# ScalarE's rounding of each activation bank put ahead of VectorE's sums of it, with conversions in other slots and some turned rows put off

## The chip, the core and the metric

The kernel runs on one core of one Trainium2 chip. The metric is device microseconds of one execution; the profiler's span, from the first to the last instruction, is a little shorter. Five engines work side by side, each with its own queue in program order: PE (TensorE, matmuls), DVE (VectorE), ACT (ScalarE), POOL (GpSimd) and SP (SyncE, which here only issues DMAs).

## The reference

Three layers follow one another, on 4 batches of 448 tokens of width 768, all in 32-bit floats:

```python
attn = sigmoid(q @ k.T / 8 - log(448)); x = attn @ v              # 12 heads of 64
u  = x + (x.T @ U @ V).T                                          # rank 32
x2 = u + max(u @ w_ch1, 0) @ w_ch2                                # 768 -> 3072 -> 768
th = x2 @ w_theta
y  = w_tok_r @ (x2 * cos(th)) + w_tok_i @ (x2 * sin(th))
out = (x2 + y) + max((x2 + y) @ moe2_w_ch, 0)
```

The weights arrive as 64-bit floats and are turned into 32-bit ones on the chip. Each product of 32-bit operands is made of three passes over rounded high parts and the remainders (low parts): high by high, high by low, low by high. So every operand of TensorE needs a high part, made by ScalarE (`hi_act`, L111, or the `relu` in L862), and a low part, a subtraction on GpSimd (`lo_pool`, L114) or VectorE (`lo_dve`, L120).

## The kernel before

The change lies in the middle layer, `max(u @ w_ch1, 0) @ w_ch2`. The hidden width of 3072 is cut into NB = 12 blocks `i` of 256 channels (two halves `n` of 128), and the batches into two pairs `pr` (batches `2*pr + t`, t = 0 or 1). A phase (i, pr) does two things at once, in seven slots k = 0 to 6. It fills four banks `g` of PSUM with `u @ w_ch1` (24 `fill` calls of three matmuls each, lines L841 to L843, in the order (t, n) = 10, 11, 00, 01), and it does the second product for the phase before it, in `seven`: one product of nine matmuls (L895 to L897) per slot, in Strassen's form with seven products in place of eight. Between them the operands are the activations `a11`, `a12`, `a22` (tiles `h_..a`), their sums `s1` to `s4` (tiles `h_..s`, from the temporary tiles `A` and `B`), and the weights `b11`, `b21`, `b22` and their sums `t1` to `t4`.

TensorE's order is written out: `first_half` calls `after(k)` (the product of slot k), then three to five fills, then `do(i, pr, k)`, the weight conversions that the table `units` gives to the slot. In slot 6 `do` comes ahead of the fills. When a bank `g` is full, `post_10`, `post_11`, `post_00` or `post_01` evacuates it. ScalarE and VectorE never read one bank at the same time: the program puts the two in their order of emission and a semaphore between them.

The products are accumulated in two PSUM tiles `acc_a` and `acc_d` of three banks, which VectorE adds to the result `X` in SBUF (L903, 1344 columns). At k = 0 the new product is also the start of a second sum: ScalarE copies it to the other tile (L918), and the product of k = 1 accumulates there. That product also reads `a12`, which is the bank filled last in the phase before.

A weight conversion (`Conv`) has the steps `size` (ScalarE), three `words` steps on VectorE (L153, L157, L163), and a finish of its own: for `w_ch1` high and low parts; for half of `w_ch2` four sums on VectorE (L258 to L261) and the parts; for `th` two VectorE instructions (L196, L199); for `wc` four subtractions on VectorE (L324 to L327). `place` and `place_extra` give each step its slot (-1 is the last slot of the phase before, 7 and up belong to the next phase). `extra` are conversions that a later layer needs, one per phase: six `th`, six `wc`, seven `tok`. Each takes one of three buffers `ca`.

In the last block (i = 11) the finished parts of `X` are turned for the next layer: `turn` transposes 128x448 elements on VectorE into a staging tile `stg` (L966), which is again one of the three buffers `ca`, and issues a DMA from GpSimd to DRAM (L967). `load_xn` (L1193) reads them back from SP's queue. After the last phase `seven_last` does the last seven products with no fills between them; then come the turned rows of batch 3 (six more, in other buffers) and `project`, the product with `w_theta`, column block c after column block c. Its operand for c = 2, the tile `xl_2`, is made by VectorE (L120) behind all of those turned rows.

Of the kernel before, what the change touches and what calls it, by code (L numbers as in the profile page):

```python
# [15 lines left out]
ALU = mybir.AluOpType  # L16
# [8 lines left out]
def tile_kernel(  # L25
# [16 lines left out]
    B, H, S, D = q.shape  # L42
    DM = H * D
    R = moe_U.shape[1]
    DF = moe_w_ch1.shape[1]
    P = 128
# [181 lines left out]
    def conv_w2(i, n):  # L228
        def dma(s):
            loader().dma_start(  # L230
                out=s.rearrange("p (j c) t -> p j (c t)", j=FB),
                in_=w2_w[i * FB * P:(i + 1) * FB * P, 2 * n * HN:2 * (n + 1) * HN].rearrange("(j p) x -> p j x", p=P),
            )
        name = f"w2_{i}_{n}"
        raw = jobs2.setdefault(i, [])

        def operand(x, home, a):
            w2_t[i, x] = o = ring_op(home, f"w2_{i}_{x}")
            hi_act(o[:, 0], a)
            return o[:, 1], a, o[:, 0]  # L240

        def fin(a, t):
            names = [f"b{j + 1}{n + 1}" for j in range(FB)]
            homes = names if i else [f"t{2 * n + j + 1}" for j in range(FB)]
            los = [operand(x, home, a[:, j * HN:(j + 1) * HN]) for j, (x, home) in enumerate(zip(names, homes))]
            yield
            for lo in los:
                lo_late(*lo)
        if i and n:
            t2 = []  # L250

            def quads():
                return [f(q.A)[:, j * HN:(j + 1) * HN] for q in raw for j in range(FB)]

            def sums():
                b11, b21, b12, b22 = quads()
                t2.append(late["c"].tile([P, HN], F32, tag="t2", name=f"t2_{i}"))
                nc.vector.tensor_sub(b11, b12, b11)  # L258
                nc.vector.tensor_sub(t2[0], b11, b22)
                nc.vector.tensor_sub(b12, b22, b12)  # L260
                nc.vector.tensor_add(b21, b21, t2[0])  # L261

            def ops(*names):
                def go():
                    t1, t4, t3, b22 = quads()
                    got = dict(t1=t1, t2=t2[0], t3=t3, t4=t4, b22=b22)
                    for lo in [operand(x, x, got[x]) for x in names]:
                        lo_pool(*lo)
                return go
            job = Conv(name, P, DM, dma, None, more=[sums, ops("t2", "t1"), ops("t3", "b22", "t4")])  # L270
        else:
            job = Conv(name, P, DM, dma, fin)
        raw.append(job)
        return job
# [382 lines left out]
    def place(i, pr, name, job, *when):  # L657
        queue(name, job)
        size, words, *rest = when
        for k in (size, words, words, words, *rest):  # L660
            ph = 2 * i + pr + k // NT7
            units.setdefault((ph // 2, ph % 2, k % NT7), []).append(name)
        assert len(job.steps) == 4 + len(rest)

    def place_extra(i, pr, k0, k1, k2):
        name, job = extra.pop(0)
        more = (k2,) if len(job.steps) == 5 else (k2, k2 + 1) if len(job.steps) == 6 else (k2, k2 + 1, k2 + 3, k2 + 4)
        place(i, pr, name, job, k0, k1, *more)

    for i in range(NB):  # L670
        if i:
            place(i, 0, ("w2", i, 0), conv_w2(i, 0), -1, 0, 2)
            place(i, 0, ("w2", i, 1), conv_w2(i, 1), 0, 1, 4, 5, 6)
            if extra:
                place_extra(i, 0, 2, 3, 6)
        if i == L:
            break
        place(i, 1, ("w1", i + 1, 0), conv_w1(i + 1, 0), 0, 1, 2)
        place(i, 1, ("w1", i + 1, 1), conv_w1(i + 1, 1), 1, 2, 6)
        if i and extra:  # L680
            place_extra(i, 1, 3, 4, 6)
# [175 lines left out]
    def max0(out, src, in1, op):  # L857
        nc.vector.scalar_tensor_tensor(out=out, in0=src, scalar=0.0, in1=in1, op0=ALU.max, op1=op)  # L858
# [32 lines left out]
    def product(o, i, pr, a, b, start):  # L891
# [5 lines left out]
            nc.tensor.matmul(o[:, e], wl, h[:, 0], start=False, stop=True, skip_group_check=True)  # L897
        h_free((i, pr, a))

    def add(i, pr, t, n, o, final):  # L900
        b = 2 * pr + t
        x = X[:, n * K3:(n + 1) * K3, b * S:(b + 1) * S]
        nc.vector.tensor_add(x, o, x)  # L903
        if final and i == L and b < B - 1:
            for d in range(n * K3, (n + 1) * K3):
                turn(b, d)

    seeded = []

# [59 lines left out]
    def turn(b, d):  # L969
        turn_x(b, d, cv.tile([P, DM], F32, tag="ca", name=f"stg_{b}_{d}", bufs=3))  # L970
# [17 lines left out]
        nc.scalar.activation(temp("A", i, pr), g, AF.Relu)  # L988

    def post_11(i, pr, g):  # L990
        max0(temp("B", i, pr), g, part["A"], ALU.add)
        relu((i, pr, "a22"), g)
        split_s(i, pr, "s1", "B", lo_pool)

    def post_00(i, pr, g):
        max0(part["A"], g, part["A"], ALU.subtract)
        max0(part["B"], g, part["B"], ALU.subtract)
        relu((i, pr, "a11"), g)
        split_s(i, pr, "s2", "B", lo_pool)

    def post_01(i, pr, g):
        max0(part["B"], g, part["B"], ALU.add)
        relu((i, pr, "a12"), g)

    ORDER = ((1, 0, post_10), (1, 1, post_11), (0, 0, post_00), (0, 1, post_01))

    def first_half(i, pr, after):

        def fills():
            for t, n, post in ORDER:  # L1010
                g = bank_g(f"{i}_{pr}_{t}{n}")
                for c in range(NK):
                    fill(i, pr, t, n, *divmod(c, K3), g)
                    if c == NK - 1:
                        post(i, pr, g)
                    yield
        todo = fills()
        for k, n in enumerate((5, 3, 3, 3, 3, 3, 4)):
            after(k)
            if k == 6:  # L1020
                do(i, pr, k)
            for _ in range(n):
                next(todo)
            if k < 6:
                do(i, pr, k)

    def phase(i, pr, prev):
        last = (i, pr) == (L, 1)

        def after(k):  # L1030
            if prev[0] == 0:
                if k < 6:
                    Y(*prev, *divmod(k, K3), lambda e2: None)
                return
            seven(*prev, k)
            if k == 0:
                split_s(*prev, "s3", "A", lo_dve)
            if k == 1:
                split_s(*prev, "s4", "B", lo_pool)
            if last and k == 6:  # L1040
                load_th(1)
                split_x(0)
        first_half(i, pr, after)
        if last:
            load_th(2)
# [95 lines left out]
    def tail(k):  # L1141
        if k == 0:
            split_s(*prev, "s4", "B", lo_pool)
        elif k == 1:
            split_s(*prev, "s3", "A", lo_dve)
            load_th(3, "b11", "t1")
            split_x(1)
        elif k == 3:
            load_th(4, "t2", "b22")
        elif k == 5:  # L1150
            load_th(5, "t3", "b21")
    seven_last(*prev, tail)
    c_st.close()
    s_st.close()
# [493 lines left out]
```

## Time and profile before

| | us |
|---|---|
| median of 3 runs | 1169.35 (1168.2 to 1170.58) |
| the profiled execution, its own time | 1169.59 |
| its span | 1167.8 |
| TensorE (matmul) busy | 1104.8, 95% of the span |
| VectorE busy | 888.3, 76% |
| ScalarE busy | 465.7, 40% |
| GpSimd busy | 413.4, 35% |

A busy share is an average over layers with different limits. The middle layer's phases run from about 240 us to 891 us of the span: those that carry `th` up to 406, those that carry `wc` up to 599, those that carry `tok` up to 794, and the rest behind them. TensorE's idle time, 63 us in all, lies mostly in the first two of these. The mean granted clock of TensorE over the span is 0.981.

### The profile page before, as it was taken

The page shows a single profiled execution, that of the slowest core. Times are in us where ns is not written, and L with a number is a line of the kernel's source. Part 1 is how long each engine was busy: PE and PEld are TensorE (multiplying, and loading weights), DVE is VectorE, ACT ScalarE, POOL GpSimd, SP SyncE. Part 2 cuts the span into 40 slices and gives each one's busy share as a digit, 9 for nine tenths or more (in the row PEclk, how much of TensorE's full clock was granted, in tenths as well). Part 3 has the DMA queues.
Part 4 walks back from the last instruction along what each step waited for, and adds up shares of the span by engine and source line. Part 5 has one row for each costly group of instructions (what it writes and reads, how often), then busy time and mean ns, then how long its engine had stood idle before and what let it go on. Part 6 is the DMA issues. An engine that isn't in the chain of part 4 may idle for free.

```text
span 1167.8 us, 16419 instructions
## 1 busy us (share of the span) xinstructions
PE 1104.8 (95%) x6165; PEld 962.8 (82%) x6165; DVE 888.3 (76%) x1127; ACT 465.7 (40%) x724; POOL 413.4 (35%) x409
## 2 busy tenths in 40 slices
PE   8999988999898999888899999999998999999997
PEld 5455567988787888787788999999987999999997
DVE  5788775588787898888888888887777663644884
ACT  6787752223333323333333333334311632542330
POOL 6421125132333243344444343434332332230373
PEclk9999998999999999999999999999999999999999
DMA  9998422123232324334243323232038432080433
GB/s 167 153 181 144 100 70 86 55 83 126 68 130 82 108 95 135 122 108 138 81 139 99 110 86 98 77 112 70 28 127 255 122 48 34 10 275 28 95 62 75
DMA packets 219919, 122.06 MB, mean 105 GB/s; under 512 B 166064, under 2 KB 205424, under 8 KB 219712
## 3 DMA queue, kind: packets, MB, share of 16 engines
q1 hardware_dynamic: 207728, 99.68, 33.5%
q0 software_dynamic: 8256, 20.87, 6.4%
q8 instruction: 48, 0.79, 0.3%
q10 hardware_dynamic: 3856, 0.48, 0.3%
q14 instruction: 31, 0.25, 0.1%
HBM read 91.23 MB, written 28.38 MB: 102 GB/s over the span
## 4 chain that ended last, share of the span: by engine, by line
PE 50%; DVE 36%; issue 6%; ACT 5%; SPq 2%; DMA 1%; POOL 1%; DVEq 0%; POOLq 0%; ACTq 0%
DVE X L903 12%; PE av L563 3%; DVE ws_w L157 3%; PE sc L529 3%; PE y L1296 3%; PE y L1294 3%; PE y L1295 3%; PE g L841 3%; DVE ws_w L153 3%; PE g L842 3%; PE g L843 3%; DVE ca_w L163 3%; PE th L1184 2%; PE th L1182 2%; PE th L1181 2%
## 5 line engine op out<-in xcount | busy, mean ns | idle before, releaser
L841 PE MATMUL g<-a,w 128*128 128x448 f32 x576 | 212.2, 368 | 3.6 <-DVE h L858 3.6
L842 PE MATMUL g<-a,w 128*128 128x448 f32 x576 | 211.5, 367 | 0.0
L843 PE MATMUL g<-a,w 128*128 128x448 f32 x576 | 211.0, 366 | 0.0
L114 POOL TENSOR_TENSOR h_s<-B,h_s 128x448 fp32r<-128x448 f32 x66 | 80.9, 1226 | 363.2 <-ACT h_s L111 363.2
L862 ACT ACTIVATE h_a<-g 128x448 fp32r<-128x448 f32 x66 | 35.8, 543 | 333.0 <-DVE B L858 295.0
L841 PEld LDWEIGHTS g<-a,w 128*128 128x128 f32 x576 | 111.0, 193 | 12.9 <-DVE h L858 3.9
L903 DVE TENSOR_TENSOR X<-acc_d,X 128x1344 f32<-128x1344 f32 x67 | 103.9, 1550 | 19.9 <-PE acc_d L897 19.8
L842 PEld LDWEIGHTS g<-a,w 128*128 128x128 f32 x576 | 110.5, 192 | 7.7
L843 PEld LDWEIGHTS g<-a,w 128*128 128x128 f32 x576 | 110.0, 191 | 7.6
L903 DVE TENSOR_TENSOR X<-acc_a,X 128x1344 f32<-128x1344 f32 x67 | 103.8, 1550 | 2.6 <-PE acc_a L897 2.0
L511 ACT ACTIVATE A<-sc,bias_s 128x896 f32<-128x896 f32 x72 | 70.0, 1015 | 14.6 <-PE sc L529 14.6
L858 DVE SCALAR_TENSOR_TENSOR h_a<-g,h_a 128x448 fp32r<-128x448 f32 x66 | 41.2, 624 | 43.9 <-ACT h_a L862 43.9
L114 POOL TENSOR_TENSOR zl<-t,zh 128x768 fp32r<-128x768 f32 x21 | 40.6, 1953 | 87.9 <-ACT zh L111 62.6
L1296 PE MATMUL y<-tok,zl 128*128 128x448 f32 x168 | 61.1, 363 | 0.0
L1294 PE MATMUL y<-tok,zh 128*128 128x448 f32 x168 | 60.8, 362 | 0.0
L1295 PE MATMUL y<-tok,zh 128*128 128x448 f32 x168 | 60.7, 362 | 0.0
L563 PE MATMUL av<-A,v 128*64 128x448 f32 x288 | 59.4, 548 | 0.7 <-ACT A L511 0.7
L163 DVE SCALAR_TENSOR_TENSOR ca_w<-ca_w,ws_w 128x768 uint32<-128x768 uint32 x48 | 56.8, 1183 | 3.8 <-DVE ws_w L157 0.5
L114 POOL TENSOR_TENSOR w<-ca_w,w 128x768 fp32r<-128x768 f32 x22 | 41.1, 1870 | 52.1 <-ACT w L111 52.1
L157 DVE SCALAR_TENSOR_TENSOR ws_w<-ca_w,ws_w 128x768 uint32<-128x768 uint32 x48 | 53.0, 1105 | 4.1
L1302 DVE TENSOR_TENSOR X<-y,X 128x448 f32<-128x448 f32 (+2 forms) x36 | 15.6, 464 | 52.3 <-PE y L1296 52.1
L1463 POOL DMA_DIRECT2D out_dram<-o x45 | 27.5, 618 | 63.4 <-DVE o L1474 60.4
(308 smaller groups left out, 2847.7 us busy)
## 6 DMA issues: line engine op xcount, KB each, us to landing
ws_w<-in_moe_w_ch_dram SPq DMA_DIRECT2D x42, 768.0 KB, 4.4
x_d<-stg POOLq DMA_DIRECT2D x24, 224.0 KB, 3.9
q<-in_q_dram SPq DMA_DIRECT2D x90, 56.0 KB, 4.3
xn<-x_d SPq DMA_DIRECT2D x52, 96.0 KB, 2.9
k<-in_k_dram SPq DMA_DIRECT2D x86, 56.0 KB, 4.4
v<-in_v_dram POOLq DMA_DIRECT2D x12, 384.0 KB, 5.0
ws_w<-in_moe_w_ch_dram POOLq DMA_DIRECT2D x6, 768.0 KB, 6.1
ws_th<-in_moe_w_theta_dram SPq DMA_DIRECT2D x6, 768.0 KB, 4.2
```

What stands on the lines that cost most here:

```text
L114: nc.gpsimd.tensor_sub(o, a, b)
L157: nc.vector.scalar_tensor_tensor(out=lw, in0=A, scalar=0x80000000, in1=lw, op0=ALU.bitwise_and, op1=ALU.bitwise_or)
L163: nc.vector.scalar_tensor_tensor(out=A if self.dest is None else self.dest(), in0=A, scalar=3, in1=lw, op0=ALU.logical_shift_left, op1=ALU ...
L511: nc.scalar.activation(a, ps, AF.Sigmoid, bias=bias_s, scale=SCALE)
L563: nc.tensor.matmul(ps[h * D:(h + 1) * D, :S], v_t[p // 2][:, 2 * (p % 2) + h, c, :], A_t[p, c][:, h, :], start=c == 0, stop=False,)
L841: nc.tensor.matmul(o, wh, xh, start=(kh, kk) == (0, 0), stop=False, skip_group_check=True)
L842: nc.tensor.matmul(o, wh, xl, start=False, stop=False, skip_group_check=True)
L843: nc.tensor.matmul(o, wl, xh, start=False, stop=(kh, kk) == (1, K3 - 1), skip_group_check=True)
L903: nc.vector.tensor_add(x, o, x)
L1294: nc.tensor.matmul(o, zh[:, sl], tok_h[:, i, :], start=first and n == 0, stop=False)
L1295: nc.tensor.matmul(o, zh[:, sl], tok_l[:, i, :], start=False, stop=False)
L1296: nc.tensor.matmul(o, zl[:, sl], tok_h[:, i, :], start=False, stop=last and n == len(slots) - 1)
```

## The change

It has five parts.

1. In `post_11`, `post_00` and `post_01` ScalarE's `relu` of the bank is emitted ahead of VectorE's sums of the same bank (`max0`); the sums are passed to `relu` as what it does in between. In `post_00` the sum `B` also comes ahead of `A`.
2. The low part of `s3` is made by GpSimd (`lo_pool`), where VectorE made it; not so in `tail`, which belongs to `seven_last`.
3. The conversions' steps take other slots: the second half of `w_ch2` goes from size 0, words 1 to size 1, words 2; the extra conversion of pair 0 from size 2, words 3, finish 6 to size 5, words 6, finish 7 (slot 0 of the next phase); the finish of the first `w_ch1` half from slot 2 to slot 3.
4. The order of the last three parts of `w_ch2` is t4, t3, b22.
5. A turned row is no longer made right behind its last sum: it goes on a list, `pending`. Two of the list are made at the end of each slot 0 to 5, and all that are left when `seven_last` has done its last sum.

```diff
-            job = Conv(name, P, DM, dma, None, more=[sums, ops("t2", "t1"), ops("t3", "b22", "t4")])
+            job = Conv(name, P, DM, dma, None, more=[sums, ops("t2", "t1"), ops("t4", "t3", "b22")])
...
-            place(i, 0, ("w2", i, 1), conv_w2(i, 1), 0, 1, 4, 5, 6)
+            place(i, 0, ("w2", i, 1), conv_w2(i, 1), 1, 2, 4, 5, 6)
             if extra:
-                place_extra(i, 0, 2, 3, 6)
+                place_extra(i, 0, 5, 6, 7)
...
-        place(i, 1, ("w1", i + 1, 0), conv_w1(i + 1, 0), 0, 1, 2)
+        place(i, 1, ("w1", i + 1, 0), conv_w1(i + 1, 0), 0, 1, 3)
...
+    pending = []
+
+    def turns(n):
+        for key in pending[:n]:
+            turn(*key)
+        del pending[:n]
...
         if final and i == L and b < B - 1:
-            for d in range(n * K3, (n + 1) * K3):
-                turn(b, d)
+            pending.extend((b, d) for d in range(n * K3, (n + 1) * K3))
...
     def post_11(i, pr, g):
-        max0(temp("B", i, pr), g, part["A"], ALU.add)
-        relu((i, pr, "a22"), g)
+        relu((i, pr, "a22"), g, lambda: max0(temp("B", i, pr), g, part["A"], ALU.add))
         split_s(i, pr, "s1", "B", lo_pool)
 
     def post_00(i, pr, g):
-        max0(part["A"], g, part["A"], ALU.subtract)
-        max0(part["B"], g, part["B"], ALU.subtract)
-        relu((i, pr, "a11"), g)
+        def sums():
+            for x in "BA":
+                max0(part[x], g, part[x], ALU.subtract)
+        relu((i, pr, "a11"), g, sums)
         split_s(i, pr, "s2", "B", lo_pool)
 
     def post_01(i, pr, g):
-        max0(part["B"], g, part["B"], ALU.add)
-        relu((i, pr, "a12"), g)
+        relu((i, pr, "a12"), g, lambda: max0(part["B"], g, part["B"], ALU.add))
...
             if k < 6:
                 do(i, pr, k)
+                turns(2)
...
             if k == 0:
-                split_s(*prev, "s3", "A", lo_dve)
+                split_s(*prev, "s3", "A", lo_pool)
...
+        elif k == 6:
+            turns(len(pending))
     seven_last(*prev, tail)
```

VectorE's queue at the end of phase (6, 0), from the evacuation of the bank `g_0_00` to that of `g_0_01`; before, with the semaphores that each row waits for:

```order
L858 SCALAR_TENSOR_TENSOR A_0_4821<-g_0_00_4886,A_0_4821 128x448 [waits PE_49]
L858 SCALAR_TENSOR_TENSOR B_0_4878<-g_0_00_4886,B_0_4878 128x448 [waits Pool_49]
L858 SCALAR_TENSOR_TENSOR h_0_a_4939<-g_0_00_4886,h_0_a_4939 128x448 [waits Activation_49]
L903 TENSOR_TENSOR X<-acc_d,X 128x3x448 [waits PE_49]
L324 TENSOR_TENSOR sp_wc_0_t<-ca_wc_0_4863 128x192 [waits DMAHW1_49]
L325 TENSOR_TENSOR sp_wc_0_t<-ca_wc_0_4863,sp_wc_0_t 128x192 [waits DVE_49]
L326 TENSOR_TENSOR sp_wc_0_t<-ca_wc_0_4863 128x192
L327 TENSOR_TENSOR sp_wc_0_t<-ca_wc_0_4863,sp_wc_0_t 128x192 [waits DVE_49]
L858 SCALAR_TENSOR_TENSOR B_0_4878<-g_0_01_4945,B_0_4878 128x448 [waits PE_49,Pool_49]
L858 SCALAR_TENSOR_TENSOR h_0_a_4998<-g_0_01_4945,h_0_a_4998 128x448 [waits Activation_49]
```

The same place of the changed kernel:

```order
L858 SCALAR_TENSOR_TENSOR B_0_4878<-g_0_00_4884,B_0_4878 128x448 [waits Activation_49,Pool_49]
L858 SCALAR_TENSOR_TENSOR A_0_4819<-g_0_00_4884,A_0_4819 128x448
L858 SCALAR_TENSOR_TENSOR h_0_a_4930<-g_0_00_4884,h_0_a_4930 128x448
L910 TENSOR_TENSOR X<-acc_d,X 128x3x448 [waits PE_49]
L153 TENSOR_SCALAR ws_wc_0_4800<-ws_wc_0_4800 128x768 [waits DMAHW6_49,DMAHW5_49]
L157 SCALAR_TENSOR_TENSOR ws_wc_0_4800<-ca_wc_0_4951,ws_wc_0_4800 128x768 [waits DVE_49,Activation_49]
L163 SCALAR_TENSOR_TENSOR ca_wc_0_4951<-ca_wc_0_4951,ws_wc_0_4800 128x768 [waits DMAHW4_49,DVE_49]
L858 SCALAR_TENSOR_TENSOR B_0_4878<-g_0_01_4938,B_0_4878 128x448 [waits Activation_49,Pool_49]
L858 SCALAR_TENSOR_TENSOR h_0_a_4989<-g_0_01_4938,h_0_a_4989 128x448
L324 TENSOR_TENSOR sp_wc_0_t<-ca_wc_0_4951 128x192 [waits DMAHW1_49,DVE_49]
```

The first sum of a bank now waits for ScalarE and the low part behind it for nothing. Between the last sum of the second product and the bank `g_0_01` the three words steps of `wc` stand where its four subtractions stood; these follow the bank.

ScalarE's queue at the same place (`w_6_..` are parts of `w_ch2`), before:

```order
L862 ACTIVATE h_0_a_4939<-g_0_00_4886 128x448 [waits DVE_49,PE_49]
L111 ACTIVATE h_0_s_4942<-B_0_4878 128x448 [waits PE_49,Pool_49]
L111 ACTIVATE w_6_t_4952<-t_6_4919 128x384
L111 ACTIVATE w_6_t_4954<-ca_w_6_0_4748 128x384
L111 ACTIVATE w_6_t_4968<-ca_w_6_1_4803 128x384
L111 ACTIVATE w_6_b_4970<-ca_w_6_1_4803 128x384
L111 ACTIVATE w_6_t_4972<-ca_w_6_0_4748 128x384 [waits PE_49]
L111 ACTIVATE sp_wc_0_b<-ca_wc_0_4863 128x768 [waits DMAHW0_49,Pool_49]
L862 ACTIVATE h_0_a_4998<-g_0_01_4945 128x448 [waits DVE_49]
```

And in the changed kernel:

```order
L862 ACTIVATE h_0_a_4930<-g_0_00_4884 128x448 [waits PE_49]
L111 ACTIVATE h_0_s_4935<-B_0_4878 128x448 [waits DVE_49]
L111 ACTIVATE w_6_t_4945<-t_6_4912 128x384
L111 ACTIVATE w_6_t_4947<-ca_w_6_0_4748 128x384
L149 ACTIVATE ca_wc_0_4951<-ws_wc_0_4800 128x768 [waits DMAHW6_49,DMAHW5_49,DMAHW4_49]
L111 ACTIVATE w_6_t_4963<-ca_w_6_0_4748 128x384 [waits PE_49]
L111 ACTIVATE w_6_t_4965<-ca_w_6_1_4828 128x384
L111 ACTIVATE w_6_b_4967<-ca_w_6_1_4828 128x384
L862 ACTIVATE h_0_a_4989<-g_0_01_4938 128x448 [waits PE_49]
```

The rounding of the bank waits for TensorE alone; ScalarE's wait for VectorE stands at the rounding of the sum `B` behind it. Behind the last row comes the copy L918 in both.

VectorE's queue at the end of `seven_last`, from the third last sum; before:

```order
L903 TENSOR_TENSOR X<-acc_d,X 128x3x448 [waits PE_49]
L903 TENSOR_TENSOR X<-acc_a,X 128x3x448 [waits PE_49]
L966 STREAM_TRANSPOSE stg_0_7488<-X 128x448 [waits DMASW2_49,DVE_49]
L966 STREAM_TRANSPOSE stg_1_7491<-X 128x448 [waits DMASW3_49]
L966 STREAM_TRANSPOSE stg_2_7494<-X 128x448 [waits DMASW4_49]
L903 TENSOR_TENSOR X<-acc_d,X 128x3x448 [waits PE_49]
L1169 MEMSET half_pi 128x1
L966 STREAM_TRANSPOSE stg_7540<-X 128x448 [waits DMASW5_49,DVE_49]
```

And in the changed kernel, from the last sum:

```order
L910 TENSOR_TENSOR X<-acc_d,X 128x3x448 [waits PE_49]
L972 STREAM_TRANSPOSE stg_4_7478<-X 128x448 [waits DMASW2_49]
L972 STREAM_TRANSPOSE stg_5_7481<-X 128x448 [waits DMASW3_49]
L972 STREAM_TRANSPOSE stg_0_7484<-X 128x448 [waits DMASW4_49]
L972 STREAM_TRANSPOSE stg_1_7487<-X 128x448 [waits DMASW5_49,DVE_49]
L972 STREAM_TRANSPOSE stg_2_7490<-X 128x448 [waits DMASW6_49,DVE_49]
L972 STREAM_TRANSPOSE stg_3_7493<-X 128x448 [waits DMASW7_49,DVE_49]
L972 STREAM_TRANSPOSE stg_4_7496<-X 128x448 [waits DMASW0_49,DVE_49]
L972 STREAM_TRANSPOSE stg_5_7499<-X 128x448 [waits DMASW1_49,DVE_49]
L972 STREAM_TRANSPOSE stg_0_7502<-X 128x448 [waits DMASW2_49,DVE_49]
L972 STREAM_TRANSPOSE stg_1_7505<-X 128x448 [waits DMASW3_49,DVE_49]
L972 STREAM_TRANSPOSE stg_2_7508<-X 128x448 [waits DMASW4_49,DVE_49]
```

Eleven turned rows now stand behind the last sum, in three staging buffers, so that from the fourth on each waits for the DMA of the row three before it. Six turned rows of batch 3 and then `xl_2` follow in both kernels; the first of the six waits for the DMA of one of the last rows (DMASW5 before, DMASW6 after, the tenth of the eleven).

## Rows read from the trace of the kernel before

**Rows 1.** The page's part 1, busy time and share of the span.

```profile
PE 1104.8 (95%) x6165; PEld 962.8 (82%) x6165; DVE 888.3 (76%) x1127; ACT 465.7 (40%) x724; POOL 413.4 (35%) x409
```

**Rows 2.** Waits of TensorE: total us, times, longest us.

```profile
PE acc_d L895 <- ACT acc_d L918: 14.6, 5, 2.9
PE acc_a L895 <- ACT acc_a L918: 9.9, 6, 2.1
PE acc_d L895 <- DVE X L903: 8.0, 7, 3.7
```

**Rows 3.** Stages: length, busy us (count) by engine, PEclk, DMA share, GB/s.

```profile
248.00:438.60 190.60, 174.11 (x810) 157.43 (x810) 162.19 (x166) 64.78 (x106) 60.57 (x47) 0.96 0.30 99
438.60:623.60 185.00, 167.92 (x786) 150.04 (x786) 161.07 (x166) 63.92 (x103) 72.47 (x51) 0.97 0.41 124
623.60:848.00 224.40, 222.77 (x1102) 206.10 (x1103) 185.00 (x206) 86.04 (x146) 89.07 (x73) 1.00 0.27 80
848.00:891.50 43.50, 38.04 (x178) 34.04 (x177) 33.38 (x39) 6.08 (x11) 12.78 (x19) 0.96 0.48 157
```

**Rows 4.** Timeline, end of phase (5, 0): start, us, engine, [idle before].

```profile
501.01 0.61 DVE L858 SCALAR_TENSOR_TENSOR B<-g,B 128x448 f32<-128x448 f32 x1
501.65 0.54 ACT L862 ACTIVATE h_a<-g 128x448 fp32r<-128x448 f32 x1 [3.46 <-DVE B L858]
502.09 1.29 ACT L918 COPY acc_d<-acc_a 128x1344 f32<-128x1344 f32 x1
503.43 0.47 PE L895 MATMUL acc_d<-h_a,w_b 128*128 128x448 f32 x1 [2.92 <-ACT acc_d L918]
```

**Rows 5.** Four us behind that wait, columns as in rows 3.

```profile
504.00:508.00 4.00, 4.00 (x14) 3.60 (x13) 2.52 (x3) 2.12 (x4) 1.15 (x1) 0.61 0.33 102
```

**Rows 6.** Groups by form: count, busy us, mean ns, idle before and its releaser.

```profile
L858 DVE SCALAR_TENSOR_TENSOR h_a<-g,h_a 128x448 fp32r<-128x448 f32 x66 | 41.2, 624 | 43.9 <-ACT h_a L862 43.9
...
L120 DVE TENSOR_TENSOR h_s<-A,h_s 128x448 fp32r<-128x448 f32 x22 | 13.9, 630 | 22.3 <-ACT h_s L111 22.3
...
L114 POOL TENSOR_TENSOR h_s<-B,h_s 128x448 fp32r<-128x448 f32 x66 | 80.9, 1226 | 363.2 <-ACT h_s L111 363.2
```

**Rows 7.** Timeline: VectorE's L153 beside GpSimd and alone; L163 alone.

```profile
383.37 1.86 POOL L114 TENSOR_TENSOR w<-ca_w,w 128x768 fp32r<-128x768 f32 x1 [3.50 <-ACT w L111]
383.80 1.85 DVE L153 TENSOR_SCALAR ws_w<-ws_w 128x768 uint32<-128x768 uint32 x1
...
392.38 0.55 DVE L153 TENSOR_SCALAR ws_th<-ws_th 128x768 uint32<-128x768 uint32 x1
...
394.04 0.96 DVE L163 SCALAR_TENSOR_TENSOR ca_th<-ca_th,ws_th 128x768 uint32<-128x768 uint32 x1
```

**Rows 8.** Timeline of the tail: VectorE's rows, then TensorE's.

```profile
886.44 1.70 DVE L966 STREAM_TRANSPOSE stg<-X 128x448 f32<-128x448 f32 x3
...
891.36 1.34 DVE L966 STREAM_TRANSPOSE stg<-X 128x448 f32<-128x448 f32 x2 [0.31 <-DMA x_d<-stg]
...
893.87 1.52 DVE L903 TENSOR_TENSOR X<-acc_d,X 128x1344 f32<-128x1344 f32 x1
...
896.04 3.28 DVE L966 STREAM_TRANSPOSE stg<-X 128x448 f32<-128x448 f32 x6 [0.64 <-DMA x_d<-stg]
902.77 0.96 DVE L120 TENSOR_TENSOR xl<-X,xh 128x768 fp32r<-128x768 f32 x1 [3.45 <-ACT xh L111]
891.55 0.33 PE L1181 MATMUL th<-th_r,xh 128*128 128x384 f32 x1
904.75 0.51 PE L1184 MATMUL th<-th_r,xl 128*128 128x384 f32 x2
```

**Rows 9.** DMAs: staging rows issued 886:892 and 898.2:901; the tok load.

```profile
DMA to landing us min/median/max: 3.9/4.1/4.8
DMA to landing us min/median/max: 3.6/10.9/12.3
tok<-tok_d SPq DMA_DIRECT2D x1, 3136.0 KB, 13.9
```

## The prediction, made before the changed kernel was timed

> **What bounds the kernel now.** I read the busy shares first, then TensorE's waits, then the stages, and last the timeline around one wait. The shares [rows 1] say that TensorE is the bound, busy 95% of the span. The waits [rows 2] say where the rest goes: in the middle layer, at the first matmul of a product, 24.5 us for ScalarE's copy of a sum (14.6 and 9.9) and 8.0 for VectorE's sums, the largest of the list. The stages [rows 3] show that a wait costs more than its idle time. From 623.6 us on, where most conversions are the small ones of `tok`, 1102 matmuls take 224.4 us, 0.2036 each; I take this as the price of a matmul without waits, though small waits are in it. At that price the 810 matmuls from 248 us on are worth 164.9 of their 190.6, the next 786 are worth 160.0 of 185.0, and the 178 of the tail 36.2 of 43.5. The excess is 25.7, 25.0 and 7.3: 58 us.
>
> VectorE is nearly as full there: 162.2 of 190.6 and 161.1 of 185.0 [rows 3]. A pair of phases has 270 matmuls (two times 63 in products and 72 in fills), so it takes 63.5 us in either stage, with 54.1 and 55.3 of VectorE's work, and TensorE needs 55.0.
>
> The timeline [rows 4] shows one wait of the costliest kind. VectorE, late with a conversion, takes its sum of the last bank of a phase at 501.01; ScalarE's rounding of that bank waits for the sum (3.46 idle), ScalarE's copy stands behind the rounding, and TensorE, which needs the copy, has been idle for 2.92 us when it resumes at 503.43. Then it runs at a granted clock of 0.61 over four us, 14 matmuls [rows 5] where the price above gives 19.6: 5.6 lost, 1.2 us, at the lower of its two clock levels (1.2 against 2.4 GHz) after an idle of 2.92 us.
>
> **The change part by part.** *Rounding first.* ScalarE's rounding of a bank no longer waits for VectorE. Both still take turns at the bank, so nothing is read faster; but the copy behind the rounding is free of VectorE's backlog. It can start when its product ends, 15 matmuls or 3.05 us before TensorE needs it, and takes 1.29 [rows 4]. I take all 24.5 us of copy waits as gone, with their low clock. VectorE gains too: its low part of each bank waited for ScalarE (43.9 us over 66 [rows 6], 0.67 each); now ScalarE is ahead, and about four us of idle time go from a pair of phases.
>
> *s3 on GpSimd.* This takes 0.63 us of work and 1.01 of waiting (22.3 over 22) off VectorE per phase, and adds 1.23 to GpSimd [rows 6], which has room (72.5 us busy of 185.0 [rows 3]). It has a price: VectorE's conversions are slowed beside GpSimd. The same L153 takes 0.55 alone and 1.85 beside a GpSimd subtraction of 1.86 [rows 7]. So the new subtraction costs VectorE between 0 and 1.23 per phase, against 1.64 gained; I take 0.6, half of it, as it meets a conversion in about every second phase. The Trainium skill speaks against this move: GPSIMD Engine Reference, 3.1 Elementwise — side-by-side cycle accounting, says that VectorE stays the rule for elementwise work, and has GpSimd 1.96 times slower. The trace has 1226 ns against 630 [rows 6], 1.95, so the ratio holds here. By that rule the move loses 0.6 us per phase; by the idle time that goes with it, it gains 1.0.
>
> *Slots.* For pair 0 VectorE's words of the extra conversion now stand where its finish stood, ahead of the last bank's sum, and the finish follows the bank. The words are not shorter: 2.5 us alone (0.55, and twice 0.96), 1.3 more where the first meets GpSimd [rows 7]; I take 4, as GpSimd makes three low parts of weights in that slot. The budget: between the end of the seventh product and the need for the bank's low part lie 12 fills' matmuls, nine of a product, 15 of fills and one more, 37 at 0.2036, 7.5 us. VectorE has in it a sum of 1.5 [rows 8], 4 of words, and 1.2 for the bank (two instructions of 0.62 [rows 6]): 6.7, if it starts in time. It starts up to 2 us late, since it comes from the bank before. [...] The later loads and the order of t4, t3, b22 I cost at nothing: the steps that use the loads stand a slot or more behind them; without that cover ScalarE would stand for a load.
>
> Sum for these: the first stage loses 25.7 less 3 times 2.0, 19.7 us; the second, of 2.9 pairs, 25.0 less 2.9 times 2.6, 17.5; the third I give 2.0, for the small waits in it. In the tail the turned rows leave VectorE's queue between the last sums, and of 7.3 excess I give 5.5. Together 44.7. Bounds: 25, if waiting for GpSimd eats what VectorE is freed of, and 58 if nothing stays.
>
> *Turned rows put off.* Here I see a loss. The order puts eleven turned rows behind the last sum, in three buffers, and behind them the six of batch 3 and `xl_2`. Before, TensorE began `project` at 891.55 and used `xl_2` at 904.75, 13.2 later; VectorE made it at 902.77, just in time [rows 8]. A buffer turned at 886.44 was turned again at 891.36: 4.92 a round [rows 8], of which its DMA takes about 4.1 [rows 9]. Eleven rows need three rounds, 14.8; the next six wait for the tenth row's DMA. That one runs beside the load of `tok` (13.9 us), and rows issued beside this load landed in 10.9 at the median [rows 9]. So this step lies between one round, 4.9, and 11.8; I take 8, as the load will have run in part. From the end of the last product: 1.5 for the sum, 14.8, 8, then 3.3 for the six and 0.95 for `xl_2` [rows 8]: 28.5, against 13.2. TensorE stands 15.3, and the low clock behind it costs 1.2 [rows 5]: 16.5. Bounds: 13.4 with 4.9, and 27 if two rounds run beside the load. What comes after is shifted, not stretched: VectorE's later work starts with `xl_2` in both kernels.
>
> Sum: 44.7 less 16.5 is 28.2. The profiled execution took 1169.59, 0.24 above the median of the runs, so I predict **1141 us**.
>
> **The rivals.** *VectorE stays the bound.* The four us that go from each pair are spent in waiting for GpSimd, as its subtraction of `s3` and the moved words meet more of GpSimd's work. Rows 7 speak for it; against it, VectorE's 54.1 and 55.3 a pair, less the 1.3 of `s3`, are no more than TensorE's 55.0. The middle layer then gains 25 and the time is 1169.6 less 25 plus 16.5, 1161. The Trainium skill's rule on this (SBUF — State Buffer, SBUF: two separate sides) is that the one of the two that starts first holds their shared ports for its whole instruction and the other blocks; 1.85 beside 0.55 [rows 7] agrees.
>
> *The turned rows cost nothing*, since their DMAs land faster. For it: one beside the load landed in 3.6 [rows 9]. Against it: even at that, four rounds of 4.5 with the 5.8 around them leave `xl_2` 10 us late. The time would be 1169.6 less 44.7, 1125.
>
> *Slower: the turned rows cost more than the middle layer gains.* All four steps go at the pace of the load itself, 13.9 to landing and 0.9 ahead of it: 59.2, plus 5.8, less 13.2, and 1.2 for the clock, 53, so 1178. It decides from 12.4 us a landing on; the longest seen is 12.3 [rows 9], and the rows would have to be slow before the load starts.
>
> **How the numbers follow.** My forecast has 0.62, VectorE as the bound 0.15, no cost of the turned rows 0.11, slower 0.06; 0.06 is left for sums of lesser gains. Within 0.2%, 2.3 us, is what a measurement of this kernel can't tell from no change; half of what is left lies there. So faster 0.91, same 0.03, slower 0.06. The forecast alone spans 1128 to 1154, by the bounds of the tail and some 8 us of the middle layer's; to leave out no more than 2 in 10 I reach to the first two rivals: 1122 to 1162.
>
> **What would show it.** Right: TensorE's waits for the copy gone; ScalarE's L862 waiting for TensorE, not VectorE; pairs of phases of 56 to 58 us in place of 63.5, at a granted clock of 1.00; one long wait of TensorE for `xl_2`, behind turned rows that wait for DMAs. Wrong: pairs still above 60 with longer L153, L157, L163 rows (the first rival); no wait at `xl_2` (the second); that wait at 40 us or more (the third). My forecast falls if VectorE's sums keep TensorE waiting in every phase, or if the turned rows' DMAs land outside of 4 to 12 us.

## The result, and the profile after

The changed kernel takes 1128.95 us (median of 4 runs, 1128.13 to 1130.13), beside it the kernel before 1168.93: a ratio of 0.9657, 95% interval 0.964 to 0.9674. The profiled execution took 1128.13, its span is 1126.4. The prediction was 1141, with a range of 1122 to 1162: faster as forecast and in the range, 12 us too slow.

The page's part 1 of the changed kernel, busy time and share of the span:

```profile
PE 1080.1 (96%) x6165; PEld 953.1 (85%) x6165; DVE 875.9 (78%) x1106; ACT 469.8 (42%) x724; POOL 439.6 (39%) x430
```

TensorE's busy time fell by 24.7 us against [rows 1] with the same 6165 matmuls; the granted clock of the stages below says why. Its waits, to be read beside [rows 2] (L924 is the copy that was L918, L910 the sum that was L903):

```profile
PE th L1192 <- DVE xl L120: 17.7, 1, 17.7
PE acc_a L882 <- DVE X L886: 4.3, 2, 3.5
PE acc_d L896 <- DVE h_a L858: 4.2, 4, 1.1
PE g L841 <- DVE h L858: 3.6, 1, 3.6
PE acc_d L895 <- DVE X L910: 3.1, 4, 1.0
...
PE acc_a L896 <- DVE h_a L858: 0.9, 3, 0.4
```

No wait for the copy is left of 24.5 us. At the top stands a new one, 17.7 us for `xl_2`; the two longest of the rest, 3.5 and 3.6, lie ahead of the first stage. The four stages of [rows 3], each between the same matmuls as there:

```profile
242.80:408.20 165.40, 163.45 (x812) 151.39 (x810) 154.21 (x157) 65.89 (x106) 68.25 (x54) 1.00 0.35 115
408.20:572.80 164.60, 159.16 (x787) 146.78 (x786) 161.16 (x165) 66.73 (x107) 84.77 (x60) 1.00 0.47 142
572.80:793.60 220.80, 220.80 (x1105) 206.95 (x1104) 179.91 (x198) 84.63 (x141) 98.28 (x80) 1.00 0.28 85
793.60:829.80 36.20, 35.38 (x176) 32.26 (x175) 28.53 (x29) 6.55 (x11) 8.67 (x12) 1.00 0.46 144
```

The granted clock is 1.00 in all four, where it was 0.96 and 0.97 in the first two and 0.96 in the last. VectorE does the same work in the second stage as before, 161 us, but in 164.6: it is 98% busy, and TensorE is idle for 5.4 of it (17.1 before). Groups by form, as in [rows 6]:

```profile
L858 DVE SCALAR_TENSOR_TENSOR h_a<-g,h_a 128x448 fp32r<-128x448 f32 x66 | 40.5, 614 | 0.0
L862 ACT ACTIVATE h_a<-g 128x448 fp32r<-128x448 f32 x66 | 35.9, 544 | 189.2 <-PE g L843 189.1
```

VectorE's low part of a bank has no idle time in front of it (43.9 before), and ScalarE's rounding waits for TensorE alone. Now the tail, VectorE's rows from the last sum on, then TensorE's at `xl_2` and the issue of `tok`; to be read beside [rows 8]:

```profile
829.99 1.56 DVE L910 TENSOR_TENSOR X<-acc_d,X 128x1344 f32<-128x1344 f32 x1 [0.36 <-PE acc_d L897]
831.47 1.69 DVE L972 STREAM_TRANSPOSE stg<-X 128x448 f32<-128x448 f32 x3
834.74 0.65 DVE L972 STREAM_TRANSPOSE stg<-X 128x448 f32<-128x448 f32 x1 [1.59 <-DMA x_d<-stg]
...
842.70 0.65 DVE L972 STREAM_TRANSPOSE stg<-X 128x448 f32<-128x448 f32 x1 [0.88 <-DMA x_d<-stg]
844.66 0.65 DVE L972 STREAM_TRANSPOSE stg<-X 128x448 f32<-128x448 f32 x1 [1.32 <-DMA x_d<-stg]
...
856.63 3.27 DVE L972 STREAM_TRANSPOSE stg<-X 128x448 f32<-128x448 f32 x6 [11.31 <-DMA x_d<-stg]
859.83 0.92 DVE L120 TENSOR_TENSOR xl<-X,xh 128x768 fp32r<-128x768 f32 x1
860.80 1.01 PE L1192 MATMUL th<-th_r,xl 128*128 128x384 f32 x2 [17.66 <-DVE xl L120]
841.66 0.94 SPq L1331 DMA_DIRECT2D tok<-tok_d  x1
```

The eleven rows pass the three buffers in 13.2 us (831.47 to 844.66), the six behind them wait 11.31 for the tenth row's DMA, issued just behind the load of `tok`, and TensorE stands 17.66 us. To add up: the starts of the same matmuls in the two profiled executions show where the changed kernel gets ahead. It is 5.1 us ahead at the start of the first stage, gains 25.3, 20.4, 4.1 and 6.9 in the four, loses 20.5 up to the first product with `tok`, and is 41.24 ahead from there to the end.

### The profile page after: what moved, and what is told of

It reads as the page before. It is cut to its first block, busy times and chain, and to the rows that moved or that the text cites. A ratio compares the mean times of both kernels' runs of the same rounds, so it can differ in the third digit from the quotient of the medians.

```text
span 1126.4 us, 16481 instructions
## 1 busy us (share of the span) xinstructions
PE 1080.1 (96%) x6165; PEld 953.1 (85%) x6165; DVE 875.9 (78%) x1106; ACT 469.8 (42%) x724; POOL 439.6 (39%) x430
## 4 chain that ended last, share of the span: by engine, by line
PE 70%; DVE 20%; issue 5%; DMA 2%; POOL 1%; SPq 1%; ACT 1%; DVEq 0%; POOLq 0%
PE g L842 7%; PE g L841 6%; PE g L843 6%; DVE X L910 6%; PE av L563 4%; PE sc L529 3%; PE y L1304 3%; PE y L1302 3%; PE y L1303 3%; PE acc_a L896 3%; PE acc_a L897 3%; PE acc_a L895 3%; PE acc_d L896 2%; PE acc_d L897 2%; PE acc_d L895 2%
## 5 line engine op out<-in xcount | busy, mean ns | idle before, releaser
L841 PE MATMUL g<-a,w 128*128 128x448 f32 x576 | 209.3, 363 | 3.6 <-DVE h L858 3.6
L842 PE MATMUL g<-a,w 128*128 128x448 f32 x576 | 209.3, 363 | 0.0
L843 PE MATMUL g<-a,w 128*128 128x448 f32 x576 | 208.9, 363 | 0.0
L910 DVE TENSOR_TENSOR X<-acc_d,X 128x1344 f32<-128x1344 f32 x67 | 104.0, 1553 | 38.0 <-PE acc_d L897 38.0
L841 PEld LDWEIGHTS g<-a,w 128*128 128x128 f32 x576 | 108.4, 188 | 12.7 <-DVE h L858 3.9
L842 PEld LDWEIGHTS g<-a,w 128*128 128x128 f32 x576 | 108.5, 188 | 7.1
L843 PEld LDWEIGHTS g<-a,w 128*128 128x128 f32 x576 | 108.4, 188 | 7.1
L910 DVE TENSOR_TENSOR X<-acc_a,X 128x1344 f32<-128x1344 f32 x67 | 103.9, 1550 | 5.5 <-PE acc_a L897 5.1
L111 ACT ACTIVATE h_s<-B 128x448 fp32r<-128x448 f32 x66 | 38.2, 579 | 148.7 <-DVE B L858 101.9
L511 ACT ACTIVATE A<-sc,bias_s 128x896 f32<-128x896 f32 x72 | 70.0, 1014 | 14.9 <-PE sc L529 14.9
L163 DVE SCALAR_TENSOR_TENSOR ca_w<-ca_w,ws_w 128x768 uint32<-128x768 uint32 x48 | 52.5, 1094 | 3.7
```

The source lines that it names most:

```text
L511: nc.scalar.activation(a, ps, AF.Sigmoid, bias=bias_s, scale=SCALE)
L841: nc.tensor.matmul(o, wh, xh, start=(kh, kk) == (0, 0), stop=False, skip_group_check=True)
L842: nc.tensor.matmul(o, wh, xl, start=False, stop=False, skip_group_check=True)
L843: nc.tensor.matmul(o, wl, xh, start=False, stop=(kh, kk) == (1, K3 - 1), skip_group_check=True)
```

## The experiments

The table has, for each kernel, the median and the lengths of five stretches between the same matmuls, read off TensorE's timeline of the one profiled execution: the four stages above, and the projection up to the first product with `tok` (31.2 is its time without waits).

| kernel | median, us | stage 1 | stage 2 | tok stage | tail | projection |
|---|---|---|---|---|---|---|
| before | 1168.9 | 190.7 | 185.0 | 224.9 | 43.1 | 31.2 |
| changed | 1128.95 | 165.4 | 164.6 | 220.8 | 36.2 | 51.8 |
| e1_turn_now | 1115.3 | 165.4 | 166.3 | 220.8 | 40.6 | 31.2 |
| e2_turns_only | 1175.1 | 189.9 | 184.6 | 224.9 | 37.0 | 46.1 |
| e3_round_first_only | 1117.9 | 164.7 | 167.9 | 220.8 | 41.3 | 32.8 |
| e4_sums_first | 1162.9 | 182.4 | 176.0 | 225.8 | 37.0 | 49.6 |
| e5_s3_vector | 1116.2 | 165.2 | 164.4 | 220.8 | 41.4 | 31.2 |
| e6_old_slots | 1118.7 | 164.7 | 168.8 | 220.8 | 41.3 | 32.0 |
| e7_tok_early | 1121.5 | 165.4 | 166.2 | 220.8 | 36.2 | 41.8 |
| e8_spread | 1119.4 | 165.4 | 167.3 | 220.8 | 42.2 | 31.2 |
| e10_low_first | 1120.5 | 167.1 | 168.6 | 220.8 | 40.2 | 31.2 |
| e11_spread_five | 1112.2 | 165.4 | 166.3 | 220.8 | 39.1 | 31.3 |
| e12_five | 1115.7 | 165.4 | 166.3 | 220.8 | 36.2 | 35.6 |
| e13_one_a_step | 1113.5 | 165.4 | 167.3 | 220.8 | 36.5 | 31.9 |

Executions of one kernel differ by 1 to 8 us (e8: 1119.03 to 1119.85, e13: 1108.03 to 1116.23), those of the kernel before, timed beside them, by 4.5 to 6.6, so medians less than 4 us apart are not told apart. The stretches are of one execution each; a clock that falls in one execution and not in another moves a stretch by up to 3 us (last section).

**One part undone or alone.** The rows turned at once again, in the changed kernel:

```diff
-            pending.extend((b, d) for d in range(n * K3, (n + 1) * K3))
+            for d in range(n * K3, (n + 1) * K3):
+                turn(b, d)
```

> The changed kernel, but each turned row issued right behind its sum, as before. My theory (putting the rows off costs TensorE a stand at xl_2 and gives only the tail's small waits back): the stand of 17.7 us is gone, the sums of the tail wait again for some 3 to 7 us, 1109 to 1116 us. Rival (putting them off pays for itself, since the sums of the last pair come sooner): 1126 to 1132 us, with waits for sums of 17 us or more in the last two phases.

Measured: 1115.33 us, ratio to before 0.9548 (0.9516 to 0.9581), so 13.6 us faster than the changed kernel. The projection is back at 31.2, the tail has 40.6 for 36.2. The rows put off cost 20.6 there and give back 4.4. My theory holds. That the medians show 13.6 of these 16.2 fits the profiles: e1's is 3.4 us behind at the start of the first stage and takes 1.7 more in the second, mostly by a clock that fell there and not in the changed kernel's (last section).

The same part alone, in the kernel before:

> The kernel before with the turned rows put off and nothing else. My theory: the stages up to the tail stay as before, the tail's sums give back some 5 us, and TensorE stands 15 to 21 us for xl_2: 1179 to 1185 us, slower than before. Rival (the stand in the changed kernel comes from TensorE being early, not from the rows): within 3 us of 1169.

Measured: 1175.05, ratio 1.0058 (1.0035 to 1.0082): slower by some 6 us, less than the 10 or more that I said. The first two stages differ from before by 0.8 and 0.4, the tail gains 6.1 and the projection loses 14.9, with TensorE standing 12.8 for `xl_2` where I said 15 to 21. So the part costs in the slow kernel too, not only because TensorE comes early; the rival falls. Most of the difference between 14.9 here and 20.6 there is which row the six wait for. VectorE's first of the six here, then the issue of the ninth of the eleven and its time to landing:

```profile
906.70 3.27 DVE L972 STREAM_TRANSPOSE stg<-X 128x448 f32<-128x448 f32 x6 [6.68 <-DMA x_d<-stg]
897.05 0.54 POOL L973 DMA_DIRECT2D x_d<-stg  x1 [0.58 <-DVE stg L972]
DMA to landing us min/median/max: 9.6/9.6/9.6
```

The ninth landed at 906.6 and the six start at once; the tenth, which they wait for in the changed kernel, landed 4.1 later. The other 1.6 of the difference is not settled.

The rounding first, alone, in the kernel before (the three `post` functions of the change and nothing else):

> The kernel before with ScalarE's rounding ahead of VectorE's sums and nothing else. My theory (the copies stood behind roundings that waited for VectorE): the 24.5 us of waits for copies and their half clock go, ScalarE's roundings wait for TensorE, and two thirds or more of the changed kernel's gain of the middle stages (46 us) come by this alone, 1129 to 1139 us. Rival (VectorE's backlog is the bound and the slots and s3 cured it): the waits only move from the copy to VectorE's sums, 1150 to 1166 us.

Measured: 1117.88, ratio 0.9568 (0.9535 to 0.9601), faster than the changed kernel and than my range. One part of five gives 51 us. TensorE's waits in this kernel (line numbers of before):

```profile
PE acc_d L895 <- DVE X L903: 7.1, 8, 3.0
PE acc_d L896 <- DVE h_a L858: 5.0, 5, 1.3
```

The copy has left the list; the waits for sums did not take its place, 7.1 us where 8.0 were [rows 2].

The reverse, all of the change but the rounding first:

> The changed kernel with VectorE's sums ahead of ScalarE's rounding again. My theory: the waits for copies come back, 1158 to 1172 us. Rival (slots and s3 alone keep VectorE on time): 1129 to 1142 us, with ScalarE's roundings waiting for VectorE at no cost to TensorE.

Measured: 1162.92, ratio 0.9952 (0.9934 to 0.9969), as my theory has it. Of its waits four lines, then ScalarE's rounding by form:

```profile
PE th L1193 <- DVE xl L120: 15.9, 1, 15.9
PE acc_d L895 <- ACT acc_d L924: 11.9, 9, 2.4
PE acc_d L895 <- ACT h_a L862: 10.6, 7, 2.2
PE acc_a L895 <- ACT acc_a L924: 4.6, 3, 2.1
L862 ACT ACTIVATE h_a<-g 128x448 fp32r<-128x448 f32 x66 | 35.9, 543 | 377.6 <-DVE B L858 377.6
```

All of ScalarE's idle time ahead of the rounding, 377.6 us, is for VectorE's sum, and the copy behind it is late again: TensorE waits 16.5 us for copies, where it waited 24.5 [rows 2]. The first two stages gain 8.3 and 9.0 us by slots and `s3`, where with the rounding first they differ by 0.9 over both stages (e3 against e1). These parts are a second remedy for the same wait, and the two don't add up.

**The small parts.** All three start from e1_turn_now. The low part of `s3` on VectorE (`lo_pool` back to `lo_dve` at k = 0):

> The kernel of e1_turn_now (1115.3 us) with the low part of s3 made by VectorE again. My theory (GpSimd takes 1.64 us a phase off VectorE and gives back at most 1.23 in slower conversions, and with the rounding first VectorE has a few us a pair to spare): 0 to 8 us slower, 1115 to 1123, the waits for VectorE's sums and low parts in the middle layer up from about 9 us. Rival, the Trainium skill's rule (GPSIMD Engine Reference, 3.1 Elementwise, side-by-side cycle accounting: VectorE stays the rule for elementwise work): 3 to 8 us faster, 1107 to 1112, since VectorE's conversions are no longer slowed. The third stage's L163 would then be shorter than in e1.

Measured: 1116.19, ratio 0.9542 (0.9525 to 0.9559), no difference from e1. The first two stages of this kernel, then of e1, columns as in [rows 3]:

```profile
243.87:409.11 165.24, 163.64 (x811) 151.34 (x810) 155.30 (x163) 66.00 (x106) 59.95 (x47) 1.00 0.35 115
409.11:573.47 164.36, 160.51 (x787) 148.27 (x786) 158.94 (x171) 66.70 (x107) 76.41 (x54) 0.99 0.47 142
```

```profile
246.20:411.62 165.42, 163.42 (x812) 151.38 (x810) 154.24 (x157) 65.93 (x106) 68.32 (x54) 1.00 0.35 115
411.62:577.89 166.27, 160.77 (x787) 148.18 (x786) 161.09 (x166) 67.04 (x107) 85.27 (x60) 0.99 0.46 141
```

VectorE does the low parts of `s3`, and in the second stage it is less busy than without them, 158.94 against 161.09, in the first 1.06 more. What GpSimd takes over there, VectorE pays in slower conversions beside it: in the second stage its three words steps take 62.5 us in this kernel and 68.0 in e1. The rival's sign came up too, in the third stage, where L163 takes 22.5 us and 25.0 in e1; it brings no time, as that stage takes 220.8 in both. The Trainium skill's rule against the move (GPSIMD Engine Reference, 3.1 Elementwise, side-by-side cycle accounting) is borne out so far that it gains nothing; the loss that it would give is not seen in the kernel's time either.

The conversions in the slots of before, with the old order t3, b22, t4:

> The kernel of e1_turn_now (1115.3 us) with the conversions in the slots and the order of before. My theory: with the rounding first the slots no longer decide which wait ends last, and round-first alone gave 1117.9, so 0 to 4 us slower, 1115 to 1119. Rival (the slots carry a gain of their own, as the 9 us a stage that sums-first kept suggest): 10 us or more slower, 1125 to 1135.

Measured: 1118.73, ratio 0.956 (0.9537 to 0.9584), as I said within what can be told from e1; the second stage is 2.5 us longer, the tail 0.7, the projection 0.8, the first stage 0.7 shorter. The tail's 0.7 goes with a clock that fell there (0.96 over the tail) and not in e1's profile (1.00).

VectorE's low part ahead of its sums of the bank, here for one of the three `post` functions and in the other two alike:

```diff
-        relu((i, pr, "a12"), g, lambda: max0(part["B"], g, part["B"], ALU.add))
+        relu((i, pr, "a12"), g)
+        max0(part["B"], g, part["B"], ALU.add)
```

> The kernel of e1_turn_now (1115.3 us) with VectorE's low part of a bank ahead of its sums of the bank, so rounding, low part, sums. Theory (what waits are left are TensorE's for the low part h_a, 5.1 us over 7): those waits go, 1110 to 1114. Rival (the sums feed ScalarE's rounding of s1 and s2 and GpSimd behind it, which become late): waits for h_s appear, 1117 or more.

Measured: 1120.52, ratio 0.9586 (0.9569 to 0.9603), slower than e1. Of its waits:

```profile
PE acc_d L895 <- DVE X L910: 9.3, 7, 3.1
PE acc_a L896 <- DVE h_a L858: 3.4, 4, 1.1
```

The waits for `h_a` fell little (5.1 to 3.9 with the one at `acc_d`, 0.5), and those for sums rose from 6.9 to 9.3. No wait for `h_s` came up: the rival had the size right and not the place. In each of two pairs with `wc` a wait of 1.0 for a sum and one of 1.06 for `h_a` in e1 became a single wait of 1.8 for the sum here, and the clock fell to 0.50 behind both (in e1 behind one). Why the sums come later is not settled.

**The turned rows.** The load of `tok` issued at the start of the last phase, which came out as 50 us earlier:

```diff
+                nc.sync.dma_start(out=f(tok), in_=tok_d)
                 load_th(0)
...
-    nc.sync.dma_start(out=f(tok), in_=tok_d)
```

> The changed kernel (1128.95 us) with the load of tok issued at the start of the last phase, 75 us earlier, not beside the turned rows. My theory (the last step, 12.0 us from the tenth row's turn to its landing, is long because the load of tok shares the DMA engines): it falls to about 4.4, as the rounds ahead of it, TensorE stands 10 us for xl_2 in place of 17.7, 1120 to 1123. Rival (the tenth row is slow by itself, or waits behind other rows' packets): 1127 to 1130.

Measured: 1121.47, ratio 0.9603 (0.9583 to 0.9622). TensorE's wait, and the landing of the last two of the eleven rows:

```profile
PE th L1193 <- DVE xl L120: 8.3, 1, 8.3
DMA to landing us min/median/max: 3.1/3.2/3.3
```

In the changed kernel the last three of the eleven, issued within 4 us of the load, land like this:

```profile
DMA to landing us min/median/max: 9.4/11.4/12.9
```

The load of `tok` was worth 9.4 us of the wait. The other 8.3 are the rounds. (The 12.0 in the expectation runs from the eleventh row's turn, 844.66, to the six; from the tenth's, 842.70, it is 13.9.)

Five staging buffers in place of three, the eleven rows still behind the last sum:

```diff
+    places = iter(range(99))
...
-        turn_x(b, d, cv.tile([P, DM], F32, tag="ca", name=f"stg_{b}_{d}", bufs=3))
+        n = next(places) % 5
+        if n < 3:
+            t = cv.tile([P, DM], F32, tag="ca", name=f"stg_{b}_{d}", bufs=3)
+        else:
+            t = cv.tile([P, DM, 2], F32, tag="ws", name=f"stg_{b}_{d}", bufs=2)
+            t = t.rearrange("p a n -> p (a n)")
+        turn_x(b, d, t)
```

> The changed kernel (1128.95 us) with five staging buffers for the turned rows in place of three, the eleven rows still behind the last sum. My theory (the rounds are bound by the number of buffers, each turned again when its DMA has landed, 4.4 us a round): two rounds and one row in place of three and two, 4 to 5 us less, 1123 to 1126. Rival (the DMAs are bound by what they can move, and five at once land later): 1127 to 1130.

Measured: 1115.71, ratio 0.9555 (0.9531 to 0.958), 13 us faster where I said 4 to 5. VectorE's last row of the eleven and the six, then TensorE, then the issue of `tok`:

```profile
840.92 0.65 DVE L973 STREAM_TRANSPOSE stg<-X 128x448 f32<-128x448 f32 x1 [0.27 <-DMA x_d<-stg]
843.95 3.28 DVE L973 STREAM_TRANSPOSE stg<-X 128x448 f32<-128x448 f32 x6 [1.52 <-DMA x_d<-stg]
848.12 1.00 PE L1199 MATMUL th<-th_r,xl 128*128 128x384 f32 x2 [2.56 <-DVE xl L120]
849.30 0.96 SPq L1338 DMA_DIRECT2D tok<-tok_d  x1
```

From the first turn (833.88) to the last the rows take 7.0 us in place of 13.2, and the eleven are issued before `tok` is, so the tenth meets no load. The two costs are not independent: whoever shortens the rounds also escapes the load. My expectation missed that.

Three buffers, two put-off rows behind each of the tail's sums from the second product on:

> The changed kernel with the put-off rows of the tail issued two at a time behind each of the tail's sums, not all eleven behind the last. My theory (the 17.7 us stand at xl_2 is a queue of eleven rows through three buffers): at most three or four rows are left behind the last sum, xl_2 is made 8 to 13 us after the last product, no stand over 2 us at xl_2, the tail's products within 2 us of the 36.2 of the changed kernel: 1108 to 1114. Rival (the stand comes from the load of tok beside the rows, not from their number): still 8 us or more at xl_2, 1118 to 1124.

Measured: 1119.44, ratio 0.9574 (0.9559 to 0.9589); the stand at `xl_2` is gone, the tail is 42.2. TensorE's waits in it:

```profile
830.63 0.44 PE L895 MATMUL acc_d<-h_s,w_t 128*128 128x448 f32 x1 [1.86 <-DVE X L910]
835.93 0.47 PE L895 MATMUL acc_a<-h_a,w_b 128*128 128x448 f32 x1 [3.24 <-DVE X L910]
```

Half right, and above my 1108 to 1114: the queue at the end goes, against the rival, but a row that waits for its buffer (2.75 us) now holds up a sum. With five buffers:

> The kernel of e8_spread (1119.4) with five staging buffers. My theory (what is left in its tail, 42.2 us against 36.2, is VectorE standing for a staging buffer ahead of a sum, 2.75 us, and the half clock behind TensorE's wait of 3.2): those waits go, the tail is 36 to 38, no stand at xl_2: 1111 to 1114, the fastest so far. Rival (VectorE has too much to do in the tail, whatever the buffers): 1116 to 1120.

Measured: 1112.17, ratio 0.9523 (0.9496 to 0.9549), as I said, with no stand at `xl_2`; the tail is 39.1, though, not 36 to 38. And with five buffers, one row a step from the third product on, seven behind the last sum:

> The changed kernel with five staging buffers and one put-off row behind each of the tail's sums from the third product on, seven rows behind the last sum. My theory (two rows a step fill VectorE in the tail, 39.1 us in e11_spread_five; eleven rows at its end make xl_2 late, 35.6 us of projection in e12_five; between the two both fit): the tail is 36 to 37.5 us, the projection 31.2 to 32, together 2 to 4 us less than in either: 1108 to 1112. Rival (the seven rows and the six behind them still land late): 1112 to 1116, with a stand at xl_2.

Measured: 1113.47, ratio 0.9506 (0.9481 to 0.953), above my 1108 to 1112. Tail and projection are as expected, 36.5 and 31.9, 2.0 less together than in e11; the median doesn't show it, as five executions went from 1108.03 to 1116.23. The last two, e1, e5 and e12 lie 53 to 57 us below the kernel before and 13 to 17 below the changed one; among them the medians don't decide.

## Why the prediction was right, and what was off

*Rounding first* held: the copy waited because it stood behind a rounding that stood behind VectorE's sum (e4's rows), and this alone is the gain (e3). What I mis-sized is the waits that stay. I took 2.0 us a pair in the first stage and 2.6 in the second, and no run shows these figures: by my own price of a matmul the first stage keeps 0.5 us of excess (0.2 a pair), the second 4.6 (1.6 a pair). In the changed kernel the waits of TensorE in these stages include:

```profile
326.61 0.47 PE L896 MATMUL acc_a<-h_a,w_b 128*128 128x448 f32 x1 [0.26 <-DVE h_a L858]
381.28 0.47 PE L896 MATMUL acc_a<-h_a,w_b 128*128 128x448 f32 x1 [0.25 <-DVE h_a L858]
...
489.39 0.47 PE L896 MATMUL acc_d<-h_a,w_b 128*128 128x448 f32 x1 [1.06 <-DVE h_a L858]
545.88 0.48 PE L896 MATMUL acc_d<-h_a,w_b 128*128 128x448 f32 x1 [1.06 <-DVE h_a L858]
```

A pair with `th` takes 54.7 us (326.61 to 381.28) with 0.25 of waits, one with `wc` 56.5 (489.39 to 545.88), where I said 56 to 58. So the first stage gave 25.3 for my 19.7, the second 20.4 for 17.5. Of the 20.4 about 1.7 is this one execution's: e1, e7, e11 and e12 do the same work there, each with one fall of the clock at 548 to 553 us that the changed kernel's profile lacks, and take 166.2 to 166.3. The late start of VectorE in its slot, which I put at up to 2 us, leaves a wait of 0.25.

*s3 on GpSimd and the slots*: I gave `s3` a gain of one us a phase; with the rounding first it is none that can be measured (e5), and the slots have at most some 3 us (e6). They were not the source of the sum.

*The tok stage and the tail's sums* gave 4.1 and 6.9 for 2.0 and 5.5. *Before 248 us* I counted nothing; it gave 5.1. Of that 2.8 lie between 211.5 and 248, where e1 has 2.8 and e3 2.3 as well; the rest, in the profiled execution, is a clock that did not fall (below).

*Turned rows put off* were a loss as I said, by the mechanism that I said: 20.5 us for 16.5. From the first turn to the eleventh's they took 13.2 (14.8), from there to the six 12.0 (8): I took a price between none and the whole of meeting the load of `tok`, and the tenth row needed 12.9 to land, the whole of it. The half clock behind the stand cost 2.9 (20.5 less 17.66), not 1.2 (1.1 by the prediction's own 5.6 matmuls); 860 to 864 has 0.50 and the next four us 0.69:

```profile
860.00:864.00 4.00, 3.20 (x10) 3.20 (x11) 3.93 (x5) 1.33 (x2) 1.52 (x3) 0.50 0.76 277
864.00:868.00 4.00, 4.00 (x18) 4.00 (x17) 2.37 (x4) 3.90 (x6) 0.00 (x0) 0.69 0.00 0
```

Together the terms were short by 5.6, 2.9, 2.1, 1.4 and 5.1, and too kind to the rows by 4.0: 13.1, which is the 41.24 of the profiles less 28.2. The medians give 40.0. That the sum is not further off is in part luck, as the rows' error goes against the others. Some 4 us of the 41.24 (2.3 before the first stage, 1.7 in the second) come of the clock in this one execution; the other three took up to 2 us longer.

*The rivals.* VectorE as the bound fell: it is 98% busy in the second stage and TensorE still takes 56.5 a pair. But its three words steps take 68.2 us there for 63.6 before, as that rival had it, and it is next in line. The rows at no cost fell by e1, the rows as a net loss too, since the wait at `xl_2` was 17.7 and not 40. One sign against my forecast did come up, landings outside of 4 to 12 us: the eleven rows took 2.2 to 12.9. Quick landings ahead of the load and slow ones beside it left the sum of the steps near, 25.2 for 22.8.

## What to carry to other kernels

When a wait names one engine, look at what stands ahead in that engine's queue: here the copy was late because of a rounding, and the rounding because of an order between two readers of a bank, and turning that order round gave more than the whole change. Work that is put off behind the last sum of a stage is not off the path if the next stage stands behind it in the same queue: count buffers, rounds, and what else the DMA engines carry at that moment. Two remedies for one wait don't add up, so try each alone before keeping both.

## What was not expected of the hardware

The same wait is followed by a low clock in one execution and not in another. At 192 us in both the changed kernel and e1 TensorE has just waited 3.47 us for VectorE, with the same work behind it. Two stretches of the changed kernel, then of e1:

```profile
192.00:196.00 4.00, 3.71 (x18) 3.49 (x19) 2.16 (x3) 0.00 (x0) 3.56 (x4) 1.00 0.70 197
196.00:200.00 4.00, 4.00 (x21) 3.75 (x20) 0.79 (x2) 0.55 (x1) 0.00 (x0) 1.00 0.00 0
```

```profile
192.00:196.00 4.00, 3.03 (x8) 2.73 (x9) 1.91 (x2) 0.00 (x0) 4.00 (x4) 0.50 0.70 189
196.00:200.00 4.00, 4.00 (x14) 3.57 (x14) 1.09 (x1) 0.00 (x0) 0.20 (x1) 0.64 0.02 8
```

39 matmuls against 22 in eight us, a granted clock of 1.00 (the level of 2.4 GHz) against 0.50 (that of 1.2) and 0.64; up to 211 us it cost e1 2.7 us. All fourteen profiled kernels have this wait, of 3.46 to 3.48 us, and the changed kernel's is the only profile in which the clock stayed at 1.00 behind it. Nor does the length of a wait settle it: 1.74 us at 247.90 of the kernel before is followed by 0.61 over 248 to 252, 2.98 us at 827.97 of e1 by 1.00 over 828 to 832. The clock goes with the spread of the runs: of e1's four, two took 1113.1 and 1113.4 at a mean clock of 0.992 and 0.994, two 1117.2 and 1118.7 at 0.988. So a profile's gain of 2 or 3 us in a stretch with such a wait may be chance until another execution shows it. What decides it no run here shows.
